# Nyström attention with a gated feed-forward: B's normalization, transpose and block forms recorded ahead of C's exponentials in the late batches, and the need of n put later

## The chip, the cores and the metric

The kernel runs on one core of a Trainium2 chip. The metric is the time of one execution on the device in microseconds (us), lower is better. Each comparison was made on one chip, with the runs of both kernels in alternating rounds.

## The reference

```python
def _attn_ref(q, k, v):                      # batch 8, heads 8, sequence 576, head size 64
    m = 32
    q_lm = q.reshape(B, H, m, S // m, D).mean(axis=3)
    k_lm = k.reshape(B, H, m, S // m, D).mean(axis=3)
    A  = softmax(scale * q    @ k_lm.T)      # 576 x 32 per head
    Bm = softmax(scale * q_lm @ k_lm.T)      # 32 x 32
    C  = softmax(scale * q_lm @ k.T)         # 32 x 576
    Z = Bm.T / (norm_1(Bm) * norm_inf(Bm) + 1e-6)
    for _ in range(6):
        Z = 2 * Z - Z @ Bm @ Z
    return A @ Z @ C @ v

def _moe_ref(x, w_gate, w_val, w_out):       # 4608 x 512 -> 4608 x 1536 -> 4608 x 512
    gate = 1 / (1 + exp(-(x @ w_gate)))
    return (gate * (x @ w_val)) @ w_out
```

(The inputs are random with a fixed seed.)

## The kernel before

The Python program is a list scheduler of its own. Every stage of every batch is a generator; a recorder chooses among them by a cost formula for each engine, and what it chooses is the fixed order of instructions on the chip. A stage says with `need(...)` what data and how many of the eight PSUM banks its next matmuls want. At run time nothing is reordered: each engine goes through its list, and a matmul that comes before its data makes TensorE wait.

```python
class Timed:                      # passes an instruction on and counts its cost
    ...
            if self.name == "act":
                busy, after = 0.05 + n * 0.00083 + 0.1 * (len(outs) - 1), 0.15
            ...
            else:                 # VectorE
                small = all(x.dtype == BF16 for x in [out, *aps.values()])
                busy, after = 0.065 + n / (1920.0 if small else 960.0), 0.12
```

The stage that the change touches, for batches 3 to 7 (`TURN` is 3, `LATE` is 2):

```python
    def mid(b):
        ...
        # bs = B's scores (TensorE); E = exp(bs) (ScalarE)
        act.activation(out=E, in_=bs, func=AF.Exp, scale=scale2)
        ...
        if b < TURN:
            ...                                   # C's scores sc, in the other layout
        else:
            for g in range(2):
                yield need(banks=2, tile='sl')
                c_rows(g)                         # sl = C's scores, 4 banks; cl = exp(sl), ScalarE
            ct = sb.tile(...)
            yield need(cl)
            turn(ct, ct, cl, ...)                 # transpose of C by a DMA
            turned_c[b] = ()
        dve.tensor_reduce(out=rs, in_=E, axis=AX.X, op=ALU.add)
        dve.reciprocal(out=rr, in_=rs)
        for g in range(2):
            if b < LATE:
                dve.tensor_scalar_mul(out=Bc[:, g, :], in0=E[:, g, :], scalar1=rr[:, g:g + 1])
            else:
                act.mul(out=Bc[:, g, :], in_=E[:, g, :], mul=rr[:, g:g + 1])
        dve.transpose(out=Bt..., in_=Bc...)
        ...
        spread(bdT, Bt)                           # block-diagonal form, two tensor_mul on VectorE
        ...
        yield need(Bc, banks=1)
        mm(out=n1, lhsT=blk, rhs=Bc, ...)         # "n" in the profile: sums for the norm
        ...
        yield need(bdT, banks=apart)
        for g in range(2):
            mm(out=s0[g], lhsT=bdT[:, g], rhs=bdT[:, g], ...)        # "s"
        s_at = [each(b, g).mul(sy[:, g, 0:128], s0[g], rc[:, g:g + 1]) for g in range(2)]
        spread(bd, Bc)
        ...                                       # sa = A's scores, aexp = exp(sa)
        # later: cv = C's value product from ct; sy's last 64 columns = cv scaled, on VectorE

    def newton(b):
        ...
            for it in range(ITERS):
                yield need(sy, banks=1)
                pn = bank(...)                    # "pn": one Newton product, two halves
                for g in range(2):
                    mm(out=pn[:, g, :], lhsT=sy[:, g, 0:128], rhs=sy[:, g, lo:128 + D], ...)
```

The rest of TensorE's work is the feed-forward: gp and vp (288 columns, first layer, one pair of each for a piece), op (512 columns, second layer) and up (weights folded with the attention's small matrix). th = tanh on ScalarE and ht = the gate product on VectorE give the banks of gp and vp back. idle_ps are dummy matmuls, set at the start where the recorder foresees a wait. GpSimd adds up the landmark sums (s_3k and so on).

The softmax here doesn't subtract the row's maximum and nothing guards it: scores larger than these inputs give would overflow.

Of the kernel before, what the change touches and what calls it, by code (L numbers as in the profile page):

```python
# [8 lines left out]
BF16 = mybir.dt.bfloat16  # L9
# [165 lines left out]
def kernel(ctx, tc, q, k, v, moe_w_gate, moe_w_val, moe_w_out, out):  # L175
# [17 lines left out]
    NC = S // P6  # L193
# [17 lines left out]
    TURN, LATE = 3, 2  # L211
# [7 lines left out]
    sb = ctx.enter_context(tc.tile_pool(name="sb", bufs=2))  # L219
# [4 lines left out]
    model = Model(BANKS)  # L224
# [4 lines left out]
    def bank(shape, dtype, name, hold=False):  # L229

        return model.take(ps.tile(shape, dtype, name=name, tag="p", bufs=BANKS), hold)
# [20 lines left out]
    def need(*data, banks=0, tile=None):  # L252


        return data, banks, None if tile is None else DEFER[tile]
# [91 lines left out]
    square_of, turned_c = {}, {}  # L347
# [27 lines left out]
    def turn(t, out, src, in_):  # L375

        nc.sync.dma_start_transpose(out=out, in_=in_)
        return model.turn(src, t)
# [147 lines left out]
    def mid(b):  # L526
# [20 lines left out]
        else:  # L547

            cl = sb.tile([128, 2, NC, 128], BF16, name=f"cl_{b}", tag="cexp", bufs=2)
# [4 lines left out]
        def row_scores(what, g, lm, o, x):  # L554

            s = [bank([128, HF], FP32, f"{what}_{b}_{g}{c}") for c in range(2)]
            for i in range(NP):
                for c in range(2):
                    r = slice(64 * c, 64 * c + 64)
                    mm(  # L560
                        out=s[c][32 * i:32 * i + 32, :],
                        lhsT=lm[r, 2 * i + g, o * c:o * c + m],
                        rhs=x[r, 2 * i + g, :], start=True, stop=True,
                    )
            return s

        def c_rows(g):
            for c, x in enumerate(row_scores("sl", g, bq, m, kT)):
                act.activation(
                    out=cl[:, g, 3 * c:3 * c + 3, 0:P6], in_=x.rearrange("p (c x) -> p c x", c=3),  # L570
                    func=AF.Exp, scale=scale1, accum_out=csl[:, g, c:c + 1])

        def c_scores(i):
            sc = bank([P6, 2, 3, 2 * m], FP32, f"sc_{b}_{i}")
            for g in range(2):
                for c in range(3):
                    mm(
                        out=sc[:, g, c, :], lhsT=kT[:, 2 * i + g, c * P6:(c + 1) * P6],
                        rhs=bq[:, 2 * i + g, :],
                        start=(g + c == 0), stop=(g + c == 3),  # L580
                    )
            cexp_at[i] = act.activation(
                out=cexp[:, :, :, i, :],
                in_=sc.rearrange("p g c (x l) -> p (c x) g l", x=2), func=AF.Exp, scale=scale1)
# [21 lines left out]
        if b < TURN:  # L606
            for i in range(2):
                yield need(banks=1)
                c_scores(i)
        else:  # L610
            for g in range(2):
                yield need(banks=2, tile='sl')
                c_rows(g)
            ct = sb.tile([128, 2 * NC, 128], BF16, name=f"ct_{b}", tag="ct", bufs=1)
            yield need(cl)
            turn(ct, ct, cl, cl.rearrange("p g c x -> p (g c x)"))
            turned_c[b] = ()
        rs = sb.tile([128, 2], FP32, name=f"rs_{b}", tag="rs")
        dve.tensor_reduce(out=rs, in_=E, axis=AX.X, op=ALU.add)
        rr = sb.tile([128, 2], FP32, name=f"rr_{b}", tag="rr")  # L620
# [1 line left out]
        Bc = sb.tile([128, 2, m], BF16, name=f"Bc_{b}", tag="Bc")  # L622
# [10 lines left out]
        def spread(dst, src):  # L633
            for g in range(2):
                dve.tensor_mul(
                    out=dst[:, g], in0=blk, in1=src[:, g, None, :].to_broadcast([128, NP, m]))

        spread(bdT, Bt)
        for i in range(2, NP if b < TURN else 0):
            yield need(banks=1)  # L640
            c_scores(i)


        yield need(Bc, banks=1)
        n1 = bank([128, 2, m], FP32, f"n1_{b}")
        mm(out=n1, lhsT=blk, rhs=Bc, start=True, stop=(b > 0))
        if b == 0:
# [377 lines left out]
    def mids():  # L1025
        for b in range(B):
            yield made(lm_of, b)
            if b > 2:
                yield step(b - 2)
            yield from mid(b)  # L1030
# [131 lines left out]
```

## Time and profile before

| | before |
|---|---|
| time, median of 3 runs (us) | 272.87 (272.48 to 273.0) |
| span of the profiled run (us) | 270.4 |
| TensorE, VectorE, ScalarE busy | 96%, 71%, 59% |

TensorE is nearly always busy, so the argument is about waits of 0.1 to 0.8 us. These can't be read from busy time, since the records of successive matmuls overlap (an op is listed as 0.38 us long, yet the next one starts after 0.216). Two views help. The timeline shows starts: in steady stretches of the trace the next matmul starts 0.216 us after one of 512 columns and 0.123 us after one of 288, which is 0.417 ns a column plus 2.5 ns; anything beyond is lost. The second is worked out from the same starts: **lost time**, the start of a matmul less the streaming time of all useful matmuls recorded before it (dummies are not useful). Where both kernels have done the same work, the difference of their lost times is the difference of the clock. For matmuls in tile modes I used one fixed figure for each kind in all kernels, so a lost time is not zero for a perfect kernel; only differences count. Some op records are missing from the traces (33 of 444 in each); they were bridged with the recorded order.

### The profile page before, as it was taken

The page shows a single profiled execution, that of the slowest core. Times are in us where ns is not written, and L with a number is a line of the kernel's source. Part 1 is how long each engine was busy: PE and PEld are TensorE (multiplying, and loading weights), DVE is VectorE, ACT ScalarE, POOL GpSimd, SP SyncE. Part 2 cuts the span into 40 slices and gives each one's busy share as a digit, 9 for nine tenths or more (in the row PEclk, how much of TensorE's full clock was granted, in tenths as well). Part 3 has the DMA queues.
Part 4 walks back from the last instruction along what each step waited for, and adds up shares of the span by engine and source line. Part 5 has one row for each costly group of instructions (what it writes and reads, how often), then busy time and mean ns, then how long its engine had stood idle before and what let it go on. Part 6 is the DMA issues. An engine that isn't in the chain of part 4 may idle for free.

```text
span 270.4 us, 7867 instructions
## 1 busy us (share of the span) xinstructions
PE 260.3 (96%) x3017; PEld 165.8 (61%) x3050; DVE 192.7 (71%) x541; ACT 158.3 (59%) x411; POOL 96.3 (36%) x107
## 2 busy tenths in 40 slices
PE   8899999999999999999999999999999999999994
PEld 5779678656674566466746656375544765467443
DVE  3377899966798679867888578696667787589311
ACT  3466768956547763766548673587527872388201
POOL 8523233950874049230591319540491100000000
PEclk9999999999999999999999999999999999999999
DMA  6999999999694999739997599939935061230143
GB/s 92 181 207 205 205 205 207 203 204 202 126 203 98 157 196 145 157 60 195 193 172 158 79 207 165 218 82 178 167 98 119 0 99 41 81 79 0 39 105 92
DMA packets 62645, 38.00 MB, mean 141 GB/s; under 512 B 33552, under 2 KB 58128, under 8 KB 62608
## 3 DMA queue, kind: packets, MB, share of 16 engines
q0 software_dynamic: 23600, 18.88, 47.0%
q1 hardware_dynamic: 38896, 18.52, 33.0%
q8 instruction: 24, 0.39, 0.6%
q14 instruction: 13, 0.11, 0.1%
q10 hardware_dynamic: 112, 0.10, 0.1%
HBM read 37.75 MB, written 9.44 MB: 174 GB/s over the span
## 4 chain that ended last, share of the span: by engine, by line
PE 89%; DMA 3%; ACT 2%; issue 2%; DVE 1%; POOL 1%; ACTq 0%; POOLq 0%
PE op L244 33%; PE gp L244 18%; PE vp L244 17%; DMA qn<-in_q_dram 3%; PE pn L244 2%; PE cv L244 2%; PE idle_ps L244 2%; PE rb L244 2%; PE sa L244 1%; PE tp_q L249 1%; PE up_2g L244 1%; PE sc L244 1%; PE up_0g L244 1%; PE up_1g L244 1%; PE tp_k L249 1%
## 5 line engine op out<-in xcount | busy, mean ns | idle before, releaser
L244 PE MATMUL op<-wo_sb,ht 128*128 128x512 bf16 (+1 forms) x411 | 108.0, 373 | 2.8 <-issue 1.9
L152 ACT ACTIVATE th<-gp 128x288 bf16<-128x288 f32 x192 | 76.5, 416 | 39.6 <-PE gp L244 30.2
L152 DVE SCALAR_TENSOR_TENSOR ht<-th,vp 128x288 bf16<-128x288 bf16 x192 | 82.4, 450 | 21.8 <-ACT th L152 15.0
L244 PE MATMUL gp<-an,U 128*128 128x288 bf16 x384 | 78.6, 286 | 0.5 <-ACT th L152 0.3
L244 PE MATMUL vp<-an,V 128*128 128x288 bf16 x384 | 78.6, 286 | 0.1
L244 PEld LDWEIGHTS <-ht 128*128 128x128 bf16 x444 | 39.4, 98 | 30.0 <-issue 8.1
L244 PEld LDWEIGHTS <-U 128*128 128x128 bf16 x384 | 35.7, 98 | 25.5 <-issue 4.0
L244 PEld LDWEIGHTS <-V 128*128 128x128 bf16 x384 | 37.5, 98 | 9.9 <-DVE V L152 0.3
L152 ACT ACTIVATE ob<-op 128x512 f32<-128x512 f32 (+1 forms) x30 | 17.7, 589 | 36.0 <-PE op L244 30.5
L152 DVE SCALAR_TENSOR_TENSOR sy<-sy,pn 128x384 bf16<-128x384 bf16 x35 | 19.3, 550 | 4.7 <-PE pn L244 4.5
L152 DVE TENSOR_SCALAR ob<-op 128x512 f32<-128x512 f32 (+2 forms) x8 | 4.9, 608 | 16.4 <-PE op L244 16.4
L244 PE MATMUL pn<-sy 128*128 128x192 bf16 (+1 forms) x84 | 13.2, 237 | 0.0
L244 PE MATMUL idle_ps<-idle_w 128*128 128x256 bf16 x61 | 11.7, 324 | 1.2 <-DVE idle_w L294 1.2
L152 DVE TENSOR_TENSOR an<-aexp,rb 128x384 bf16<-128x384 bf16 (+1 forms) x32 | 12.6, 446 | 0.2 <-PE rb L244 0.2
L244 PEld LDWEIGHTS <-sy 128*128 128x128 bf16 x88 | 8.0, 97 | 6.3 <-DVE sy L152 3.7
L152 ACT ACTIVATE aexp<-sa 128x288 bf16<-128x288 f32 x32 | 10.6, 417 | 1.5 <-PE sa L244 1.1
L244 PEld LDWEIGHTS <-WT 64*32 64x32 bf16 x384 | 3.8, 89 | 9.4 <-issue 6.9
L267 POOL DMA_DIRECT2D kn<-in_k_dram x9 | 7.0, 781 | 5.1 <-PE py L244 2.5
L267 POOL DMA_DIRECT2D vn<-in_v_dram x8 | 6.3, 791 | 5.9 <-PE gp L244 2.5
L244 PEld LDWEIGHTS <-idle_w 128*128 128x128 bf16 x61 | 6.4, 115 | 2.9 <-DVE idle_w L294 1.2
L152 DVE CAST U<-up_0g 128x512 bf16<-128x512 f32 x8 | 5.5, 689 | 3.7 <-PE up_0g L244 3.4
L152 ACT ACTIVATE cl<-sl 128x288 bf16<-128x288 f32 x20 | 8.0, 410 | 0.1
(183 smaller groups left out, 349.3 us busy)
## 6 DMA issues: line engine op xcount, KB each, us to landing
vn<-in_v_dram POOLq DMA_DIRECT2D x8, 576.0 KB, 9.3
kn<-in_k_dram POOLq DMA_DIRECT2D x7, 576.0 KB, 8.3
qn<-in_q_dram POOLq DMA_DIRECT2D x7, 576.0 KB, 13.4
out_dram<-ob SPq DMA_DIRECT2D x53, 64.0 KB, 3.3
out_dram<-ob SPq DMA_DIRECT2D x17, 192.0 KB, 2.6
out_dram<-ob SPq DMA_DIRECT2D x18, 128.0 KB, 2.4
wg_sb<-in_moe_w_gate_dram POOLq DMA_DIRECT2D x3, 512.0 KB, 20.4
wv_sb<-in_moe_w_val_dram POOLq DMA_DIRECT2D x3, 512.0 KB, 20.8
```

The costliest lines, as they stand in the source:

```text
L152: f(**kw)
L244: nc.tensor.matmul(**kw)
L249: nc.tensor.transpose(**kw)
L267: nc.gpsimd.dma_start(out=t[:, hs], in_=src[b, hs].rearrange("h (p c) d -> p h (c d)", p=P6))
```

## The change

The intent: in the late batches B's chain of small steps (row sum, reciprocal, Bc, transpose, bdT) shall not wait behind C's four long exponentials, so that the matmuls n and s on Bc and bdT find their data ready. The need of n is also put 0.25 us later, in batches 1 to 7.

```diff
@@ in mid(b)
-        else:
-            for g in range(2):
-                yield need(banks=2, tile='sl')
-                c_rows(g)
-            ct = sb.tile([128, 2 * NC, 128], BF16, name=f"ct_{b}", tag="ct", bufs=1)
-            yield need(cl)
-            turn(ct, ct, cl, cl.rearrange("p g c x -> p (g c x)"))
-            turned_c[b] = ()
         rs = sb.tile([128, 2], FP32, name=f"rs_{b}", tag="rs")
         ...
         spread(bdT, Bt)
+        if b >= TURN:
+            for g in range(2):
+                yield need(banks=2, tile='sl')
+                c_rows(g)
+            ct = sb.tile([128, 2 * NC, 128], BF16, name=f"ct_{b}", tag="ct", bufs=1)
+            yield need(cl)
+            turn(ct, ct, cl, cl.rearrange("p g c x -> p (g c x)"))
+            turned_c[b] = ()
         ...
-        yield need(Bc, banks=1)
+        yield need(model.landed[Bc.name] + (0.25 if b else 0.0), banks=1)
```

## The prediction

> **What bounds the kernel now.** I read the page first, then the wait list of TensorE, then the timeline around the operations that the change moves. From the page of the kernel before (section 1: busy us, share, instructions; section 4: the chain that ended last):
>
> ```profile
> PE 260.3 (96%) x3017; PEld 165.8 (61%) x3050; DVE 192.7 (71%) x541; ACT 158.3 (59%) x411; POOL 96.3 (36%) x107
> ...
> PE 89%; DMA 3%; ACT 2%; issue 2%; DVE 1%; POOL 1%; ACTq 0%; POOLq 0%
> ```
>
> TensorE is busy 96% of 270.4 us and is 89% of the chain. Next, TensorE's list of waits (total us, times, longest):
>
> ```profile
> PE op L244 <- issue: 1.9, 12, 0.2
> PE idle_ps L244 <- DVE idle_w L294: 1.2, 1, 1.2
> PE tp_q L249 <- DMA qn<-in_q_dram: 0.8, 2, 0.6
> PE gp L244 <- ACT th L152: 0.3, 1, 0.3
> ```
>
> Nothing here names B or C. But busy time overlaps for pipelined matmuls, so a short stall hides inside "busy". I therefore compared start times: in steady stretches a 512-column matmul (op) starts 0.216 us after the one before, a 288-column one (gp, vp) 0.123 us. Whatever exceeds that is lost. The timeline of batch 4, first ScalarE and VectorE, then TensorE (start, length, what), shows the place that the change aims at:
>
> ```profile
> 120.55 0.22 ACT L152 ACTIVATE E<-bs 128x64 f32<-128x64 f32 x1 [0.44 <-PE bs L244]
> 120.70 0.41 ACT L152 ACTIVATE cl<-sl 128x288 bf16<-128x288 f32 x1
> ...
> 121.86 0.42 ACT L152 ACTIVATE cl<-sl 128x288 bf16<-128x288 f32 x1
> ...
> 123.95 0.53 ACT L152 ACTIVATE Bc<-E,rr 128x32 bf16<-128x32 f32 x2 [0.97 <-DVE rr L152]
> ```
> ```profile
> 123.44 0.21 DVE L152 TENSOR_REDUCE rs<-E 128x2 f32<-128x64 f32 x1
> 123.69 0.17 DVE L152 RECIPROCAL rr<-rs 128x2 f32<-128x2 f32 x1
> 124.51 0.24 DVE L152 STREAM_TRANSPOSE Bt<-Bc 128x64 bf16<-128x64 bf16 x1 [0.66 <-ACT Bc L152]
> 124.79 0.36 DVE L152 TENSOR_TENSOR bdT<-blk,Bt 128x128 bf16<-128x128 bf16 x2
> ```
> ```profile
> 124.16 0.38 PE L244 MATMUL op<-wo_sb,ht 128*128 128x512 bf16 x1
> 124.53 0.19 PE L244 MATMUL n<-Bc,blk 128*128 128x64 bf16 x1
> ```
>
> B's exponential E ends at 120.77, yet its row sum rs starts only at 123.44: the four exponentials of C (cl) and two gate products stand between. Then the matmul n waits for Bc: op should free the array at 124.16 + 0.216 = 124.37, n starts at 124.53, 0.05 us after Bc ends (124.48). That is 0.16 us lost with everything behind it in TensorE's order. The kernel records its instructions in a fixed order by its own cost formulas, and these take Bc to be ready earlier than it is.
>
> The same reading for batches 1 to 7 gives stalls ahead of n of 0.146, 0.292, 0.286, 0.160, 0.159, 0.287 and 0.234 us, sum **1.56 us**, and ahead of the matmuls on bdT (s) 0.102, 0.000, 0.026, 0.028, 0.083, 0.028 and 0.000, sum **0.27 us**. In each batch n starts about 0.05 us after Bc's end. So at most 1.83 us, 0.7% of 272.87, can be won here.
>
> **What the Trainium skill says.** (1) "TensorE: Matmul & The Clock Gate", section "Wait — 56ns, not 53.3ns?": warm matmuls start N / 2.4 GHz plus some 2.5 ns apart. The trace agrees: 216 and 123 ns against 215.8 and 122.5. (2) Same page, section "Architectural detail: the array is 16× 32×32, not 1× 128×128": ScalarE and VectorE take their work strictly first in, first out. The trace agrees: Bt kept VectorE idle 0.66 us above. So the place in the recorded order decides. (3) "TensorEngine Tiling (Array Packing)", section "Key Properties": a change of tiling mode drains TensorE. The trace agrees: a matmul that follows one of another tile mode (op to bs, vp to sa, upv to gp) starts 0.09 us late, nearly always.
>
> **The change part by part.** I compared the built orders of both kernels; the arithmetic is the same.
>
> *n is asked for 0.25 us later* in batches 1 to 7 (the new term in its need), and in batches 3 to 7 it also comes after all exponentials of C. In the new order batch 4 has, from sl on: 8 op and 8 gp or vp matmuls ahead of n, 8 x 0.216 + 8 x 0.123, so n comes some 2.7 us after sl (before: 3.7). Bc is then ready about 1.2 us after sl (below). The stall of n should vanish in 3 to 7 (1.13 us) and nearly so in 1 and 2 (0.44). In batches 4 to 7 s now follows n directly, which is safe since bdT is ready 0.8 us after Bc. Together **-1.75 us**, allowing 0.08 for remnants.
>
> *More filler.* While no half of the first hidden layer is done, the recorder fills waits that it foresees with dummy matmuls (idle_ps). Their count goes from 61 to 66, all in batch 1's part. One takes 0.11 us from start to start in the trace (15.71, 15.82, 15.93): **+0.55 us**, on the path.
>
> *Tile-mode switches.* Counted in the orders: 96 before, 98 after, because sa and cv, adjacent before in batches 4 and 5, now stand apart. 2 x 0.09 = **+0.2 us**.
>
> *C's exponentials come later.* ScalarE's order in 3 to 7 is now E, Bc, Bc, then cl. From the durations above, counted from the start of bs (120.27): E ends at 0.50; rs at 0.57; rr 0.25 later; Bc 0.26 after that; both Bc 0.44 (123.95 to the next th at 124.39); so the first cl starts at about 1.5 instead of 0.43, and ScalarE gives back the four PSUM banks of sl at about 2.0, 2.4, 2.8, 3.2, all 1.1 us later. VectorE also stands still for Bt while the gate products wait behind it. The order of bank reuse in the new program shows who takes these banks: in batch 4 op at some 1.8 us, so 0.2 us of waiting; in batches 3, 5 and 7 gp and vp at about their release, so 0 to 0.1; in batch 6 only half of sl is issued at first. My estimate is 0.06 us a batch, **+0.3 us**. The kernel's own formulas count a Bc as 0.077 us where the trace has 0.22 to 0.27, which is why I allow up to 1 us.
>
> *The transpose of C* (ct) is issued about 1.1 us later and lands 4.0 to 5.9 us after its issue. cv, which needs it, stands some 9.7 us of TensorE work after sl in four of five late batches (before 8.0 to 9.2), so it is still hidden. The tail is the same in both orders: 84 op matmuls after the last gate.
>
> Sum: 272.87 - 1.75 + 0.55 + 0.2 + 0.3 = **272.2 us**, 0.3% faster.
>
> **The rivals.**
> *Bank wait takes the stall's place.* The four banks that C holds 1.1 us longer stop gp, vp and op. For it: half of the eight banks are held, and ScalarE's real Bc is longer than the recorder believes. Against it: the recorder sees most of the delay and puts op matmuls, which need one bank, into it. If each late batch lost 0.3 us: 273.4.
> *A new latency chain becomes the bound*: later ct, later cv, later Newton steps, and TensorE runs out of ready work. Against it: TensorE always has gates of the batch before and op tiles, and waits for cv nowhere now. If it happened in the first late batches, 1 to 2 us: 274.
> *The whole gain arrives*: filler merely replaces waits that were there anyway in the start-up (0.42 us before a gp near 40 us, for instance), and banks cost nothing: 271.1.
> *Earlier B shortens the latency to the next batch and so the whole pipeline.* Against it: 96% busy; nothing on TensorE waits for that latency. I give it little.
>
> **Range and chances.** No rival reaches 2% (5.5 us): the stalls sum to 1.83 us, and the costs I see to about 2. The three runs before spread 0.5 us. I take 271.1 to 273.4 as the range, and 0.98 for within 2%.
>
> **What would show it.** Right: n starts directly after its predecessor in all late batches; Bt waits for Bc as before, but 2 to 3 us earlier relative to bs; 66 idle_ps; TensorE's sum of busy time lower by about 1 us in the windows of batches 3 to 7 and higher by 0.5 before 55 us. Wrong: waits of gp, vp or op on cl or th in TensorE's list, of cv on ct, or a start-up longer by more than 1 us.

## The result, and the profile after

| | before | after |
|---|---|---|
| time, median (us) | 272.87 (272.48 to 273.0) | 274.53 (274.35 to 274.53) |
| ratio | | 1.0062, 95% interval 1.0039 to 1.0085 |
| span of the profiled run (us) | 270.4 | 272.4 |

The changed kernel is slower by 0.6%. The time lies outside the predicted range.

The page of the changed kernel, busy us and the chain that ended last:

```profile
PE 262.2 (96%) x3022; PEld 166.3 (61%) x3055; DVE 195.5 (72%) x543; ACT 157.7 (58%) x409; POOL 96.0 (35%) x107
...
PE 87%; DVE 3%; ACT 3%; DMA 3%; issue 2%; POOL 1%; ACTq 0%; POOLq 0%
```

TensorE stays at 96%, but VectorE and ScalarE now hold 6% of the chain in place of 3%: TensorE waits for them more often. Batch 4 around the place of the change, ScalarE, then TensorE:

```profile
120.71 0.22 ACT L152 ACTIVATE E<-bs 128x64 f32<-128x64 f32 x1
121.48 0.53 ACT L152 ACTIVATE Bc<-E,rr 128x32 bf16<-128x32 f32 x2 [0.55 <-DVE rr L152]
121.92 0.39 ACT L152 ACTIVATE cl<-sl 128x288 bf16<-128x288 f32 x1
...
123.07 0.41 ACT L152 ACTIVATE cl<-sl 128x288 bf16<-128x288 f32 x1
...
123.45 0.42 ACT L152 ACTIVATE th<-gp 128x288 bf16<-128x288 f32 x1
```
```profile
123.56 0.41 PE L244 MATMUL vp<-an,V 128*128 128x288 bf16 x2
123.80 0.19 PE L244 MATMUL n<-Bc,blk 128*128 128x64 bf16 x1
123.83 0.28 PE L244 MATMUL s<-bdT 128*128 128x128 bf16 x2
```

The intent is met: n starts at 123.80, directly after vp, 1.8 us after Bc ended. The price is on ScalarE too: the first exponential of C starts 0.99 us after E ended (121.92 against 120.93), and the next th only at 123.45.

Lost time on TensorE by stretches of the program, from the two profiles:

| stretch, from the first matmul named to the next | before | after | difference |
|---|---|---|---|
| start to bs of batch 1 (the same instructions in all kernels here) | 15.54 | 15.67 | +0.13 |
| bs of batch 1 to bs of batch 2 | 5.42 | 5.74 | +0.32 |
| bs to sa of batch 2 | 0.91 | 0.64 | -0.27 |
| sa of batch 2 to bs of batch 3 | 1.16 | 1.83 | **+0.67** |
| bs of batch 3 to the first gp of batch 7 | 8.98 | 10.16 | **+1.18** |
| the rest | 0.23 | 0.23 | 0 |
| sum | 32.23 | 34.26 | +2.03 |

The difference of the spans is the same 2.0 us. The first stretch varied from 15.1 to 16.2 between the profiles with identical instructions, which is noise of the start; the other stretches agreed to about 0.05 us wherever the orders were the same. And by what TensorE was about to run in the fifth stretch, batches 3 to 7:

| lost ahead of ... (us) | before | after |
|---|---|---|
| n | 1.13 | 0.01 |
| s, and the matmul after s | 0.52 | 0.76 |
| gp, vp (with a wait of 0.18 ahead of an op in batch 4, after) | 0.05 | 0.48 |
| pn | 0.28 | 1.23 |
| changes of tile mode, and inside tiled blocks | 7.00 | 7.62 |
| the rest | 0.00 | 0.06 |
| sum | 8.98 | 10.16 |

So n's 1.12 us were won, as the change intended, and 2.3 us were lost elsewhere. Three places of it can be seen in the timeline.

*Banks.* Batch 5, TensorE and ScalarE of the changed kernel:

```profile
155.90 0.19 PE L244 MATMUL n<-Bc,blk 128*128 128x64 bf16 x1
156.20 0.27 PE L244 MATMUL s<-bdT 128*128 128x128 bf16 x2
156.50 0.40 PE L244 MATMUL gp<-an,U 128*128 128x288 bf16 x2
```
```profile
155.35 0.41 ACT L152 ACTIVATE cl<-sl 128x288 bf16<-128x288 f32 x1
...
155.73 0.72 ACT L152 ACTIVATE th<-gp 128x288 bf16<-128x288 f32 x2
```

By the rate above, a 64-column matmul such as n frees the array after 0.03 us, and bdT had been ready since 154.96, but s starts 0.30 us after n. By the order of bank reuse s takes the bank of a gp whose th stands behind C's four exponentials on ScalarE and ends at about 156.15.

*The first Newton product.* Batch 4, before and after (start, length of the pair of halves); then VectorE after:

```profile
130.84 0.33 PE L244 MATMUL pn<-sy 128*128 128x192 bf16 x2
```
```profile
131.34 0.56 PE L244 MATMUL cv<-vn,ct 96*32 96x64 bf16 x48
131.83 0.68 PE L244 MATMUL rb<-rt,sel 80*128 80x128 bf16 x10
132.43 0.50 PE L244 MATMUL pn<-sy 128*128 128x192 bf16 x2
```
```profile
132.04 0.59 DVE L152 TENSOR_SCALAR sy<-cv,rcs,rc 128x64 bf16<-128x64 f32 x2
```

The pair takes 0.50 us for 0.33: its second half waits for the second scaling of cv, which ends at 132.63. In the new order pn stands closer behind cv: between the last cv and pn lie 0.5 to 0.7 us of TensorE's work in place of 0.9 to 1.5 (batches 3 to 7, from the recorded orders and the rates above).

*Batch 2, VectorE, GpSimd and TensorE.* The timelines of the three engines, first after, then before:

```profile
68.25 1.76 DVE L152 TENSOR_TENSOR bd<-blk,Bc 128x128 bf16<-128x128 bf16 x2
69.93 1.17 DVE L152 SCALAR_TENSOR_TENSOR ht<-th,vp 128x288 bf16<-128x288 bf16 x3
...
68.16 1.63 POOL L152 TENSOR_TENSOR s_3k<-kT 128x768 f32<-128x768 bf16 x1 [9.95 <-DMA kT<-kn]
...
69.98 1.12 PE L244 MATMUL sa<-qT,klm 64*32 64x288 bf16 x16
```
```profile
67.83 0.35 DVE L152 TENSOR_TENSOR bd<-blk,Bc 128x128 bf16<-128x128 bf16 x2
...
68.19 1.64 POOL L152 TENSOR_TENSOR s_3k<-kT 128x768 f32<-128x768 bf16 x1 [9.90 <-DMA kT<-kn]
...
70.23 0.44 PE L244 MATMUL sa<-qT,klm 64*32 64x288 bf16 x16
```

The pair of bd multiplications takes 1.76 us for 0.35 when it starts just after an addition on GpSimd, the gate products queue behind it, and the block sa takes 1.12 us for 0.44; run 6 below tests that this is the cause. The Trainium skill, "SBUF — State Buffer", section "Who interferes with whom", says that a VectorE instruction with two SBUF inputs contends with a GpSimd instruction that reads SBUF, that the lock on their shared ports is exclusive, and that the order of issue decides who is blocked. The trace agrees: the first bd ends at 69.87, 0.08 us after the addition's end at 69.79. Before, bd was done at 68.18, 0.01 us ahead of the addition.

### The profile page after: what moved, and what is told of

It reads as the page before. It is cut to its first block, busy times and chain, and to the rows that moved or that the text cites. A ratio compares the mean times of both kernels' runs of the same rounds, so it can differ in the third digit from the quotient of the medians.

```text
span 272.4 us, 7878 instructions
## 1 busy us (share of the span) xinstructions
PE 262.2 (96%) x3022; PEld 166.3 (61%) x3055; DVE 195.5 (72%) x543; ACT 157.7 (58%) x409; POOL 96.0 (35%) x107
## 4 chain that ended last, share of the span: by engine, by line
PE 87%; DVE 3%; ACT 3%; DMA 3%; issue 2%; POOL 1%; ACTq 0%; POOLq 0%
PE op L244 33%; PE gp L244 17%; PE vp L244 16%; DMA qn<-in_q_dram 3%; PE pn L244 3%; PE cv L244 2%; DVE ht L152 1%; PE idle_ps L244 1%; PE rb L244 1%; PE sc L244 1%; PE tp_q L249 1%; PE sa L244 1%; ACT th L152 1%; PE up_2g L244 1%; PE up_0g L244 1%
## 5 line engine op out<-in xcount | busy, mean ns | idle before, releaser
L244 PEld LDWEIGHTS <-ht 128*128 128x128 bf16 x444 | 40.1, 98 | 30.5 <-issue 6.9
L152 ACT ACTIVATE ob<-op 128x512 f32<-128x512 f32 (+1 forms) x29 | 17.1, 591 | 36.1 <-PE op L244 24.5
L152 DVE TENSOR_SCALAR ob<-op 128x512 f32<-128x512 f32 (+2 forms) x9 | 5.6, 618 | 16.5 <-PE op L244 16.5
L244 PE MATMUL pn<-sy 128*128 128x192 bf16 (+1 forms) x84 | 13.9, 238 | 0.0
L267 POOL DMA_DIRECT2D qn<-in_q_dram x9 | 6.7, 747 | 3.5 <-PE up_2g L244 1.8
```

Of the source, the lines that this page charges most:

```text
L152: f(**kw)
L244: nc.tensor.matmul(**kw)
L267: nc.gpsimd.dma_start(out=t[:, hs], in_=src[b, hs].rearrange("h (p c) d -> p h (c d)", p=P6))
```

## The experiments

Theory 1: two separate costs, one of the 0.25 us (the start and the meeting in batch 2), one of the move (C's exponentials hold banks longer). Theory 2: the first Newton product's wait is a cost of its own, from the recorder's figures. Theory 3: the meeting of bd and the addition costs 0.7 us. Rivals: one part of the change makes the whole loss; or any new weave costs about 1 us, whatever is in it. All runs gave correct results. The medians of before in the three sets of rounds were 272.61, 272.55 and 272.49; the changed kernel, at its ratio of 1.0062, stands at about 274.2 there.

**1. The move alone** (e1_move_alone).

```diff
-        yield need(model.landed[Bc.name] + (0.25 if b else 0.0), banks=1)
+        yield need(Bc, banks=1)
```

> The move of B ahead of C's exponentials in batches 3 to 7, without the 0.25 us in n's need. (Its built program is the same as that with the 0.25 us kept in batches 3 to 7 only, so it also stands for that.) Lost time of TensorE is counted as start time less the streaming time of all matmuls recorded before. Theory 1, two separate costs: up to bs of batch 3 this equals the kernel before (23.0 us lost, not 23.9), since nothing before batch 3 changes, and no bd multiplication takes 1.6 us; in batches 3 to 7 the same kinds of waits as in the changed kernel (pn's second half 0.17 us each, s and op on banks of sl) outweigh the 1.1 us of n, net about +1.2 us: 273.7 us. Rival A, the 0.25 us alone is to blame: 271.8. Rival B, the move alone makes the whole loss: 274.5.

Measured 273.79, ratio 1.0043 (1.0022 to 1.0064). The number is that of theory 1, but its reasoning holds only in part. Up to bs of batch 3 it is as before (23.13 against 23.03 us lost), yet a bd did meet the addition:

```profile
L152 DVE TENSOR_TENSOR bd<-blk,Bc x16: 213/216/1660, 16.4 to 224.8; 128x128 bf16<-128x128 bf16 x16
```

(The row of the bd group in that profile: minimum, median and maximum ns.) In this order of batch 2 it cost only 0.17 us. In batches 3 to 7 it lost 9.05, only 0.07 more than before; the remaining 1.1 us were lost after the first gp of batch 7, where op had been recorded so far ahead that the last up blocks had no op between them, and gp and vp waited for VectorE to empty banks (0.92 us ahead of gp and vp there, 0.01 before). The late hand-back of sl's banks shows too, but in another place than in the changed kernel: the last matmuls of sl itself start 0.16 us late in batches 5, 6 and 7, and each takes a bank of sl's first half. So the move alone costs about 0.4%, but not in the place that I had named.

**2. The 0.25 us alone** (e2_quarter_alone): the same line added to the kernel before.

> The kernel before with n's need 0.25 us later in batches 1 to 7, nothing moved. Theory 1: up to bs of batch 3 as the changed kernel, 23.9 us lost, with one bd of batch 2 at 1.6 us beside a GpSimd addition and some 0.75 us of waits within sa of batch 2; then n's stalls of batches 3 to 7 (1.13 us) vanish with nothing in their place: 272.87 + 0.85 - 1.1 = 272.6. Rival A, the 0.25 us is the whole loss: 274.5. Rival B, it costs nothing: 271.3.

Measured 272.14, ratio 0.9989 (0.9963 to 1.0015): no different from before. By stretches it is theory 1 in detail: +0.33 from bs of batch 1 to bs of batch 2, -0.27 up to sa, +0.71 from sa of batch 2 to bs of batch 3 with one bd of 1.66 us, then 8.60 in batches 3 to 7 (n 0.34). By these stretches the 0.25 us lose 0.77 us early and win 0.38 late, a net loss of 0.4 us (0.15%), which is within the interval of the ratio. Rival A falls.

**3. Bc on VectorE** (e3_bc_on_vector): the changed kernel with

```diff
-            if b < LATE:
+            if b < LATE or b >= TURN:
                 dve.tensor_scalar_mul(out=Bc[:, g, :], ...)
```

> The changed kernel with the two Bc multiplications of batches 3 to 7 on VectorE instead of ScalarE, so that C's exponentials follow E directly on ScalarE and no longer wait for the reciprocal. Theory 1: the later hand-back of sl's banks is what makes op, s and gp wait in batches 4, 5 and 6, about 0.7 us; these go, the 0.85 us of batches 1 and 2 and the waits of pn's second half (0.17 us each) stay: 273.8. Rival: the waits come from the new weave as such and are found again elsewhere: 274.5.

Measured 272.72, ratio 1.0006 (0.9983 to 1.0029), better than expected. In batches 3 to 7 the sum was 8.80: gp, vp and op lost no more than in the kernel before, s 0.18 (in batch 5 alone), and pn about 1.6. But the recorder also knew of the change and wove anew (bd met the addition only for 0.86 us, and no wait came of it), so this run doesn't isolate the cause; run 9 does.

**4. B directly behind C's exponentials** (e4_behind_c): the kernel before with c_rows left in its place, and the `need(cl)` and `turn` put behind `spread(bdT, Bt)`.

> The kernel before with B's normalization recorded directly behind C's exponentials and ahead of the transpose's need (before: behind the transpose), without the 0.25 us. ScalarE then has E, four cl, Bc. Theory 1: batches 1 and 2 as before (23.0 us lost at bs of batch 3), C is not delayed, Bc is ready about 2.4 us after bs, n stands 1.8 us after sl and so may still stall by up to 0.3 us; pn's second half waits 0.17 us in up to three batches: 272.5 to 273.0. Rival, every new weave of the late batches costs about 1 us: 273.9.

Measured 273.69, ratio 1.0044 (1.0022 to 1.0066): a miss for theory 1, and here the rival's number. n still lost 1.31 us and pn 1.31 in batches 3 to 7: an earlier Bc doesn't help when the recorder, believing it ready earlier still, moves n up as well (in batches 3 to 6 n stands 2.1 us of TensorE's work behind the start of sl, before 3.4 to 3.9).

**5. The first Newton product later** (e5_pn_later): the changed kernel with

```diff
-                yield need(sy, banks=1)
+                yield need(model.landed[sy.name] + (0.3 if it == 0 else 0.0), banks=1)
```

> The changed kernel with the need of the first Newton product (pn, first step of batches 1 to 7) put 0.3 us later, so that the recorder sets two op matmuls ahead of it; the recorded orders are otherwise nearly the same. In the changed kernel this product's halves start 1.23 us late in batches 3 to 7 (0.28 in the kernel before), because they follow cv's scaling by VectorE (0.59 us for two) too closely. Theory 2, this is the largest new wait: it falls from 1.23 to under 0.4 and nothing takes its place: 274.5 - 0.9 = 273.6. Rival, the wait only moves to the next step of the chain: 274.5.

Measured 273.39, ratio 1.0025 (1.0001 to 1.0048), about 0.8 us below the changed kernel. pn's loss fell from 1.23 to 0.56 and the sum of batches 3 to 7 from 10.16 to 9.43; the other terms stayed within 0.1. Batch 4 in that profile, the pair at its normal 0.33 us again:

```profile
132.26 0.33 PE L244 MATMUL pn<-sy 128*128 128x192 bf16 x2
```

Part of the wait moved to the second product (0.12 to 0.19 us in batches 3 and 4), so theory 2 holds for 0.7 of its 0.9 us.

**6. bd of batch 2 early** (e6_bd_early): the changed kernel; only VectorE's order differs.

```diff
         spread(bdT, Bt)
+        if b == 2:
+            for g in range(2):
+                nc.vector.tensor_mul(out=bd[:, g], in0=blk, in1=Bc[:, g, None, :]...)   # not counted here
 ...
-        spread(bd, Bc)
+        if b == 2:
+            for g in range(2):
+                model.run("dve", [bd[:, g]], [blk, Bc], 0.065 + 128 / 1920.0, 0.12)     # counted only
+        else:
+            spread(bd, Bc)
```

> The changed kernel with the two bd multiplications of batch 2 moved on VectorE to directly behind bdT; the recorder's accounts and the orders of all other engines stay as they are. In the changed kernel's profile the first of them met a GpSimd addition and took 1.62 us for 0.22. Theory 3, the two engines get in each other's way: no bd over 0.3 us, the waits within sa of batch 2 (0.75 us) vanish, lost time from sa of batch 2 to bs of batch 3 falls from 1.83 to about 1.16 as in the kernel before: 274.5 - 0.7 = 273.8. Rival, the wait of sa has another cause: 274.5.

Measured 274.0, ratio 1.0055 (1.0034 to 1.0077): in time, not distinguishable from the changed kernel. By stretches it is clear: no long bd, and from sa of batch 2 to bs of batch 3 1.15 us lost in place of 1.83. The row of the two moved multiplications, and the block sa:

```profile
L633 DVE TENSOR_TENSOR bd<-blk,Bc x2: 217/218/219, 67.0 to 67.2; 128x128 bf16<-128x128 bf16 x2
```
```profile
70.83 0.44 PE L244 MATMUL sa<-qT,klm 64*32 64x288 bf16 x16
```

Of the 0.68 us won, 0.2 were given back ahead of sa (a vp waited 0.22 us for a gate product that now stood behind bd), 0.1 in the stretch before, and this profile had a slow start (16.21 to bs of batch 1). Theory 3 is shown for its mechanism and its 0.7 us.

**7. The 0.25 us alone, with bd early** (e7_quarter_bd).

> The 0.25 us alone (second run above, 272.14) with bd of batch 2 moved in the same way. Theory 3: from sa of batch 2 to bs of batch 3 1.16 us lost in place of 1.86, so 271.4, faster than the kernel before by 0.4%. Rival: 272.1.

Measured 272.16, ratio 0.9985 (0.9964 to 1.0005): no gain in time over run 2. The stretch after sa of batch 2 fell from 1.87 to 1.15 as expected, but 0.2 us came back ahead of sa and 0.2 in batch 1 (s waited 0.26 us there, in this profile only; why stays open).

**8. Run 3 with bd early and the first Newton product later** (e8_all_mended).

> The changed kernel with Bc of batches 3 to 7 on VectorE (third run above, 272.72), bd of batch 2 moved, and the first Newton product's need 0.3 us later. Theories 2 and 3: the waits of pn (1.22 us there) fall by 0.9, bd (0.86 us, hidden there) changes nothing or up to 0.3: 271.7. Rival, the gains don't add since the recorder sets other waits: 272.7.

Measured 272.8, ratio 1.0008 (0.9989 to 1.0026): a miss, the rival's number. pn lost 1.69 us, against some 1.6 in run 3 by the same count, so nothing was won there. (The 1.22 us of the expectation leave out 0.24 ahead of the first product in batch 7 and 0.12 ahead of the second in batch 6.) The first product no longer waited, but the recorder had set the second right behind: VectorE was still busy with earlier work (in batch 6 the normalization of A) when the first product came out, and the second waited 0.19 to 0.38 us in every late batch.

**9. Bc on VectorE, counted as ScalarE's** (e9_bc_physical): the changed kernel; the orders of TensorE, GpSimd and SyncE are identical, and those of ScalarE and VectorE differ by the ten Bc alone.

```diff
+            elif b < TURN:
                 act.mul(out=Bc[:, g, :], in_=E[:, g, :], mul=rr[:, g:g + 1])
+            else:
+                nc.vector.tensor_scalar_mul(out=Bc[:, g, :], in0=E[:, g, :], scalar1=rr[:, g:g + 1])
+                model.run("act", [Bc], [E, rr], 0.05 + m * 0.00083, 0.15)
```

> The changed kernel with the two Bc multiplications of batches 3 to 7 carried out by VectorE, right behind the reciprocal, while the recorder still counts them as ScalarE's: the orders of TensorE and of everything else stay as they are, only Bc changes its engine. Theory 1: C's exponentials start right after E (about 0.1 us after its end, not 1.0), the banks of sl come back 0.9 us sooner, so the waits ahead of gp and vp (0.48 us in batches 3 to 7), behind s (0.38) and ahead of s (0.38) nearly vanish; the wait of pn stays at 1.23: 274.4 - 1.1 = 273.3. Rival, these waits have other causes: 274.4, with the terms unchanged.

Measured 272.54, ratio 0.9998 (0.9968 to 1.0029), 1.7 us below the changed kernel, where 1.1 was expected. Batch 5, ScalarE and TensorE:

```profile
152.42 0.22 ACT L152 ACTIVATE E<-bs 128x64 f32<-128x64 f32 x1 [0.44 <-PE bs L244]
152.57 0.41 ACT L152 ACTIVATE cl<-sl 128x288 bf16<-128x288 f32 x1
```
```profile
155.32 0.19 PE L244 MATMUL n<-Bc,blk 128*128 128x64 bf16 x1
155.35 0.28 PE L244 MATMUL s<-bdT 128*128 128x128 bf16 x2
155.46 0.41 PE L244 MATMUL gp<-an,U 128*128 128x288 bf16 x2
```

C's exponentials start 0.15 us after E starts (1.21 in the changed kernel), and s follows n without a gap. In batches 3 to 7 the sum fell from 10.16 to 8.56: gp, vp and op 0.48 to 0.08, s and behind it 0.76 to 0, tiled blocks and mode changes 7.62 to 7.17. pn stayed at 1.24. With the same order of matmuls, this shows that two small ScalarE instructions ahead of C's exponentials, with their wait for the reciprocal, cost 1.6 us.

Laid side by side, the two profiles show where: nine waits, 1.54 us together, that the changed kernel has and this run hasn't. By the order of bank reuse, 0.46 us were for banks that sl had held (an op in batch 4, sl's second half and s in batch 6), and 1.08 us for banks of gp and vp (s and gp in batch 5, an op in batch 6, gp, vp and sa in batch 7). Batch 3 lost nothing.

**10. All three mended, orders kept** (e10_three_mended): runs 5, 6 and 9 together.

> The changed kernel with all three causes taken away, each in the way that leaves the recorded orders nearly as they are: Bc physically on VectorE as in the run above, bd of batch 2 early, pn's first need 0.3 us later. If the three terms are the whole loss and add up: 274.4 - 1.1 - 0.5 - 0.7 = 272.1, at or below the kernel before. Rival, something else is still missing: over 273.

Measured 271.31, ratio 0.9945 (0.9925 to 0.9966): faster than before. In batches 3 to 7 7.75 lost; 10.16 less 1.60 and 0.73 is 7.83, so the terms add. So the three causes are more than the whole loss. That the 1.5 us below the kernel before are the move's own gain is not shown: the mends of this run go beyond undoing, and run 11 reaches the same time without the move.

**11. Only later needs, batches 3 to 7** (e11_slack_late): the kernel before, nothing moved.

```diff
-        yield need(Bc, banks=1)
+        yield need(model.landed[Bc.name] + (0.35 if b > 2 else 0.0), banks=1)
 ...
-        yield need(bdT, banks=apart)
+        yield need(model.landed[bdT.name] + (0.15 if b > 2 else 0.0), banks=apart)
 ...
-                yield need(sy, banks=1)
+                yield need(model.landed[sy.name] + (0.3 if it == 0 else 0.15), banks=1)
```

> A candidate: the kernel before, nothing moved, with later needs in batches 3 to 7 alone: n 0.35 us, s 0.15 us; and for the Newton products 0.3 us (first step) and 0.15 us (other steps) in batches 1 to 7. The waits ahead of n (1.13 us in batches 3 to 7), s (0.48) and pn (0.28) go to under 0.5 in sum, batches 1 and 2 are nearly as before: 272.55 - 1.2 = 271.4. Rival, the recorder's new weave sets other waits: 272.5.

Measured 271.16, ratio 0.9946 (0.9921 to 0.9971), as expected.

**12. The same from batch 2 on** (e12_slack_all): `b > 1` in place of `b > 2`.

> The same with n's and s's later needs in batch 2 too. The 0.29 us ahead of n in batch 2 go as well, but bd of batch 2 moves later and may meet the GpSimd addition as in the changed kernel: 271.2 if it does not, 271.9 if it does (one bd over 0.8 us, and waits within sa of batch 2).

Measured 270.29 (270.16 to 270.75), ratio 0.9913 (0.9893 to 0.9933): the best, faster than both kernels, and 0.9 us better than expected. bd did not meet the addition this time (longest 221 ns). In batches 3 to 7 n lost 0.00, pn 0.18, the sum was 7.70 in place of 8.98. A further 0.39 us came from bs of batch 1 to bs of batch 2, and 0.27 ahead of sa of batch 2; run 11 had the 0.39 too. The traces of runs 11 and 12 differ by only 0.24 us of lost time (the profiled execution of run 11, 270.6 us, was the fastest of its six); the rest of the 0.87 us between the medians is unexplained. With runs 2, 11 and 12, new weaves that cost nothing or gain, the rival that any new weave costs about 1 us falls.

| lost time (us) | before | after | run 9 | run 10 | run 12 |
|---|---|---|---|---|---|
| bs of batch 1 to bs of batch 2 | 5.42 | 5.74 | 5.74 | 5.73 | 5.03 |
| bs to sa of batch 2 | 0.91 | 0.64 | 0.63 | 0.83 | 0.64 |
| sa of batch 2 to bs of batch 3 | 1.16 | 1.83 | 1.87 | 1.15 | 1.15 |
| bs of batch 3 to first gp of batch 7 | 8.98 | 10.16 | 8.56 | 7.75 | 7.70 |

## Why the prediction was wrong

What bounds the kernel and where it lost time was read rightly: the stalls ahead of n were real, and n's 1.13 us in batches 3 to 7 went to 0.01. "Within 2%" holds too. The sign and the range were wrong: the measured time is 2.3 us above the predicted (274.53 against 272.2), because costs were mis-sized or not seen.

- *n and s, -1.75 us.* For n right. For s wrong: "safe since bdT is ready" looked at the data alone. s and the matmul after it lost 0.76 us in place of 0.52, for want of a bank. (The reading of 0.27 us ahead of s was itself short: it left out the second of the two matmuls, which started 0.08 us late in each of batches 3 to 6.)
- *Filler, +0.55, and tile-mode switches, +0.2.* Counted rightly (66 dummies, 98 switches). On the path, the whole stretch of batch 1 cost 0.32: waits ahead of gp and vp fell there from 1.06 to 0.30 us, so some of the filler took the place of waits that were there anyway, as the third rival said, while other waits are new; no run isolates the filler.
- ***C's exponentials come later, +0.3 us.*** This step failed first. The mechanism was named, and the times of the hand-back (1.1 us later) were about right, but the price was mis-sized: 0.06 us a batch was said, run 9 measured 1.6 us in all, 0.32 a batch on average, which is the price that the prediction had named for its first rival and not taken. The estimate looked only at the matmuls that take sl's own banks, and for these it was not far off (0.46 us; the 0.2 us ahead of op in batch 4 came as 0.18). It left out that the th instructions wait behind the same exponentials on ScalarE, so that the banks of gp and vp come back late as well, which s, sa and the next gp want: 1.08 us.
- ***"TensorE ... waits for cv nowhere now"*** and with it the whole of the second rival's dismissal. This step failed next. cv itself was in time, as said, but what follows it was not looked at: pn stands closer behind cv in the new order, and lost 1.23 us in place of 0.28. Run 5 took 0.67 of that away (0.73 of the whole sum). That the closeness comes from cv's later place in the recorded order is read from the orders; it was not isolated. It is not C's later exponentials on the chip, for run 9 removed these and left pn at 1.24.
- *bd and the addition in batch 2, +0.67 us*, was not foreseen at all. It was 0.01 us away in the profile of the kernel before, for whoever would have laid the two engines' timelines side by side. Runs 2 and 6 show it.
- The sign that I had given for "wrong", waits of gp, vp or op in TensorE's list of waits, did not show there; that list has only gaps where the pipeline ran empty. Lost time counted from starts showed them. The promised fall of TensorE's busy time in batches 3 to 7 did not come either: it was 150.4 us there in place of 147.2.

Of the 0.62 us that tiled blocks and mode changes lost more in batches 3 to 7, run 9 did not return 0.17. That is about the size of the two added tile-mode switches of the prediction, 0.09 us each, which by the recorded orders both fall into this stretch (59 before, 61 after); no run isolates it. What stays open is the s of batch 1 in run 7, and the difference between runs 11 and 12.

## What to carry to other kernels

When a small step is pulled ahead of long ones on an in-order engine, ask not only whether its consumer gains, but what the long ones and everything queued behind them release, and who wants it. In a kernel recorded against a cost formula, mend the formula or the slack where it is wrong (run 12: 0.15 to 0.35 us on three kinds of need, 0.9% faster) before moving work. To find a cause in such a kernel, change what an engine does while the recorder's account stays the same (runs 6, 9 and 10); an experiment that lets the recorder weave anew (runs 1 to 4 and 8) measures the new weave along with the change.

## What the Trainium skill lacked or had wrong

- "TensorEngine Tiling (Array Packing)", section "Key Properties": says that a change of tiling mode drains TensorE, without a figure. Here most changes cost 0.09 us, 96 to 98 of them in the kernel.
- "ScalarE: Activation LUTs", section "What ACT_TABLE_LOAD costs": nothing is lacking here, though the recorder's formula, 0.08 us for each Bc, is far below it. An ACTIVATE with immediate scale and bias takes 186 ns plus 0.833 ns an element, a pointer operand 93 ns more, and one following another overlaps it by 93 ns: as an estimate 0.31 us for a Bc of 32 elements, and 0.21 us from one start to the next. Here the medians were 0.31 to 0.32 us, and two Bc and the next exponential started 0.22 us apart on average (121.48 to 121.92).
- "SBUF — State Buffer", section "Who interferes with whom": right as far as it goes. The runs add the size: a multiplication of 0.22 us took 1.62 to 1.66 us in five profiles, 0.86 in one, and ended 0.08 us after the addition's end in the changed kernel; how much of it reached TensorE was 0 to 0.7 us, by what was queued behind.
